# A written order of the early instructions on all five engines of a three-stage attention and mixture kernel

## The chip, the cores and the metric

The kernel runs on 1 core of one Trainium2 chip, with TensorE (PE), VectorE (DVE), ScalarE (ACT), GpSimd (POOL) and SyncE (SP, which issues the transfers). The metric is device time in microseconds of one execution. The kernel before took 881.34 us in the median of three runs (880.27 to 882.56).

## The reference: what is computed

Three stages follow each other on 3072 tokens of width 384.

```python
# 1: gated linear attention, 4 batches x 8 heads, 768 steps, head width 48
S = a * S + k v^T          # a is complex, its magnitude clipped at 0.999; S starts at 0
y = q . Re(S)
# 2: a gated product, weights 384x1536, 384x1536 and 1536x384, given in float64
x = ((y @ w_a) * (y @ w_b)) @ w_out
# 3: top-1 of 8 experts for tokens with x @ w_skip > 0
out = x + gate * (relu(x @ w1[e]) @ w2[e])
```

## The kernel before

**Units and groups.** The attention is cut into 24 units: 6 chunks of 128 steps times 4 batches. Two units make a group of 256 tokens, so that there are 12 groups. The names below carry the unit's or the group's number.

**A unit of attention** goes through `att_exp` (L195), `att_trig` (L238) and `att_pe` (L290). The first clamps `re` on DVE, takes logarithms and exponentials on ACT in the tiles `t1` and `t2`, sums them along the steps on PE (`l2`) and scales `q`, `k` and `im`. The second takes the angle (`t4`), sums it on PE (`tp`), reduces it on DVE (`t3`) and takes sine and cosine on ACT (`ts`, `t4`); products with these give `qr` and `kr` on DVE (L284, L286). The third transposes them on PE (`pq`, `pk`, copied by ACT to `tq`, `tk`), makes the masked scores (`pc`, then `sc` on DVE, L334), the change of the state (`ds`, `state`) and the output `y`. ACT and DVE write `y` as a high and a low half into `xt`, the input of the gated product (L364, L365).

**Weights of the gated product** come as float64: 18 chunks of 768 KB, `rawa0` to `rawa5`, `rawb0` to `rawb5` and `rawo0` to `rawo5`. `decode` (L371) makes float32 of a chunk with one Abs on ACT (L376) and three instructions on DVE (L377, L381, L382); `split` (L386) writes the high half on ACT (L387) and the low half on POOL (L388). Only three decode buffers go round, so that a chunk waits until the chunk three before it has been split. A one-element copy on POOL (L423) holds back the load of chunk k+3 until chunk k is decoded. Chunks of `w_out` are also transposed and multiplied by the gate's columns (`wt`, `wtt`, `w2s`).

**The gated product** of group g and slice f is `ab{g}_{f}`: 18 matmuls of 256 columns on PE (L500 to L502), then `asb` (ACT L506, DVE L507), `gh` (ACT L509), `gl` (DVE L511), and six matmuls into `op{g}_0` and `op{g}_1` (L484 to L486). Routing and the experts of stage 3 follow, and are not touched.

**What sets the order.** The string `START` says in which order the pieces of the first two groups are written down. From that the framework's scheduler puts one order on each engine, by its own estimate of durations. A table `HOLD` of 19 entries bends this: an entry such as `('tab', 2): ('tk', 0, 1)` makes one instruction (the third load of a function table) stand behind another (the copy `tk0_1`) on its engine. Each engine works through its own order strictly, and waits for data of others by semaphores.

Of the kernel before, what the change touches and what calls it, by code (L numbers as in the profile page):

```python
# [3 lines left out]

# [44 lines left out]
IM_MAX = 0.93  # L49
SPL = 4  # L50
OFF = {'add': (0, 1, 2, 3), 'k': (0, 1, 2, 3, 6), 'qs': (5, 6, 7), 'ks': (), 'im': (5,), 'kc': (5,)}
HOLD = {('tab', 2): ('tk', 0, 1), ('shl', 2): ('kr', 1), ('abs', 1): ('tk', 1, 0), ('re', 4): ('sc', 5, 0), ('mx', 3): ('qr', 2), ('shl', 5): ('sc', 3, 0), ('im', 4): ('sc', 4, 0), ('abs', 12): ('ts', 0), ('abs', 4): ('ts', 0), ('shl', 7): ('qr', 1), ('im', 5): ('qr', 5), ('abs', 15): ('tq', 5, 0), ('abs', 9): ('ts', 3), ('abs', 17): ('ts', 1), ('shl', 8): ('sc', 4, 1), ('im', 1): ('qr', 4), ('tab', 6): ('tq', 0, 1), ('tab', 3): ('tk', 5, 1), ('im', 6): ('qr', 4)}
WARMS = (10, 6, 24)
WARMX = (13, 8)
ENGINES = {getattr(mybir.EngineType, x) for x in ("PE", "Activation", "DVE", "Pool")}
# [1 line left out]
SGN = ()  # L57
WO = DM + 10
SKIP_IDX = 8192.0


def kern(tc, q, k, v, a_re, a_im, w_a, w_b, w_out, w_skip, w_gate, w1, w2, out):
    nc = tc.nc
    dve, act, pool, pe, sync = nc.vector, nc.scalar, nc.gpsimd, nc.tensor, nc.sync
    st = ExitStack()
    with st:
# [19 lines left out]
        tri_f = gpool.tile([P, P], F32, tag="xt0", name="tri_f", bufs=1)  # L86
        pool.memset(tri_f, 1.0)
        pool.affine_select(out=tri_f, in_=tri_f, pattern=[[1, P]], compare_op=ALU.is_ge, fill=0.0, base=0, channel_multiplier=-1)
        tri_r = cpool.tile([P, P], F32R, name="tri_r")
        dve.tensor_copy(tri_r, tri_f)  # L90
        tri = tri_r.bitcast(F32)
        if SPL:
            trit = cpool.tile([P, P], F32, name="trit")
            dve.tensor_scalar(out=trit, in0=tri, scalar1=INV2PI, scalar2=None, op0=ALU.mult)
        b_eps = cpool.tile([P, 1], F32, name="b_eps")
        pool.memset(b_eps, LN_EPS)
        b_tiny = cpool.tile([P, 1], F32, name="b_tiny")
        pool.memset(b_tiny, 1e-30)
        b_magic = cpool.tile([P, 1], F32, name="b_magic")
        pool.memset(b_magic, MAGIC)  # L100
        b_hpi = cpool.tile([P, 1], F32, name="b_hpi")
        pool.memset(b_hpi, math.pi / 2)
        immax = cpool.tile([P, 2 * NG], F32, name="immax")
# [30 lines left out]
        def after(later, earlier, how=mybir.DependencyClass.NoSync):  # L134
            tc.add_manual_dep(
                later, earlier.name,
                mybir.DependencyInfo(how, mybir.DependencyReason.DATA),
                reason="table order",
            )


        marks, holds = {}, dict(HOLD)

# [248 lines left out]
        wg = cpool.tile([P, NCC, 10], F32, name="wg")  # L392
# [153 lines left out]
        xd = dpool.tile([NTOK, DM], F32, name="xd")  # L546
# [127 lines left out]
        iota = cpool.tile([P, CAP], BF16, name="iota")  # L674
        pool.iota(iota, pattern=[[1, CAP]], base=0, channel_multiplier=0, allow_small_or_imprecise_dtypes=True)
        desc = cpool.tile([P, NE], F32, name="desc")
        pool.iota(desc, pattern=[[-1, NE]], base=NE, channel_multiplier=0, allow_small_or_imprecise_dtypes=True)
        ones = cpool.tile([P, P], BF16, name="ones")
        pool.memset(ones, 1.0)
        ustrict = cpool.tile([P, P], BF16, name="ustrict")  # L680
        pool.memset(ustrict, 1.0)
        pool.affine_select(out=ustrict, in_=ustrict, pattern=[[1, P]], compare_op=ALU.is_gt, fill=0.0, base=0, channel_multiplier=-1)
        ohs = cpool.tile([P, NE], BF16, name="ohs")
        pool.memset(ohs, 0.0)
        tbl = cpool.tile([P, 2 * 6 * NE], F32, name="tbl")
        pool.memset(tbl, 0.0)

        rt_c = cpool.tile([P, 2 * NG, 6], BF16, name="rt_c")
# [3 lines left out]
        rt_oh = cpool.tile([P, 2 * NG, NE], BF16, name="rt_oh")  # L692
        rt_r = cpool.tile([P, 2 * NG, 6, NE], BF16, name="rt_r")
# [3 lines left out]
        def indices(count_only=False):  # L697
# [4 lines left out]

            dve.tensor_scalar(out=gi, in0=ti[:, :, 0], scalar1=SKIP_IDX, scalar2=None, op0=ALU.add)
            dve.scalar_tensor_tensor(out=gi, in0=ti[:, :, 1], scalar=-SKIP_IDX, in1=gi, op0=ALU.mult, op1=ALU.add)
            dve.tensor_copy(siu, gi)
# [184 lines left out]
        for w in START.split():  # L890
            n = [int(x) for x in w[1:].split(".")] if w[1:] and w[0] != "d" else []
# [24 lines left out]
        for g in range(2, NG):  # L916
# [14 lines left out]
            if g >= NG - 2:  # L931
                for r in sorted(lgs):
                    route(r)

        good = cpool.tile([P, 2], F32, name="good")
        red = cpool.tile([P, 2], F32, name="red")
        cnt = cpool.tile([P, 1], F32, name="cnt")
# [114 lines left out]
        def load_value(x, most):  # L1052
            return nc.values_load(todo[0:1, x : x + 1], min_val=0, max_val=most, skip_runtime_bounds_check_because=why)  # L1053

        left = load_value(2, NTOK // CAP + 1)
        with tc.If(left != 0, label="rest"):
# [5 lines left out]
            n = load_value(0, NTOK // CAP)  # L1062
# [39 lines left out]
```

## Time and profile before

| what | value |
|---|---|
| median of three runs | 881.34 us |
| profiled execution, its own time | 882.94 us |
| span of the profiled execution | 881.0 us |
| PE busy | 829.3 us (94%) |
| DVE busy | 552.9 us (63%) |
| ACT busy | 463.6 us (53%) |
| POOL busy | 266.9 us (30%) |
| mean granted clock of TensorE | 0.98 |

The span is cut into 40 slices on the page, each of 22 us; a digit is the busy share in tenths. An idle time of an engine is put down to the instruction whose result ended it. Durations of neighbouring instructions on DVE and ACT overlap by some hundredths of a microsecond, so that their sum can exceed the busy time of a window.

### The profile page before, as it was taken

To read this page: it belongs to the slowest core of one execution; us is meant where nothing else is said; L and a number is where in the kernel's file an instruction comes from. 1 tells how busy PE (TensorE), PEld (TensorE's weight loads), DVE (VectorE), ACT (ScalarE), POOL (GpSimd) and SP (SyncE) were. 2 spreads that over 40 slices of the span, in tenths; PEclk is the share of its full clock that TensorE was granted. 3 is DMA by queue.
4 is the path that set the end of the run, shared out by engine and by line. 5 is a ranking of instruction groups with operands and counts; after the bars stand their busy time and mean duration, and the time that the engine had idled before them with its cause. 6 is when DMAs were issued, how large, how long until landed. Compare 5 with 4: busy or idle time off the path is not lost. (4 is left out here: it accounts for less than half of the span.)

```text
span 881.0 us, 19344 instructions
## 1 busy us (share of the span) xinstructions
PE 829.3 (94%) x7643; PEld 798.3 (91%) x7643; DVE 552.9 (63%) x1294; ACT 463.6 (53%) x977; POOL 266.9 (30%) x313
## 2 busy tenths in 40 slices
PE   2678879999999999999999999999999999999995
PEld 0568869999999999999999999999999989999995
DVE  4989996639476493855838558394653645655551
ACT  6768664637356472654726546374443425555540
POOL 5464570213031210313103130031201414665741
PEclk9979888999999999999999999999999999999999
DMA  9656532304122040321303222020101419766600
GB/s 217 146 159 168 164 92 54 73 11 96 33 69 51 16 103 19 73 47 47 73 19 76 44 64 56 19 74 10 47 1 41 140 49 327 246 220 215 192 14 30
DMA packets 159923, 79.23 MB, mean 90 GB/s; under 512 B 131060, under 2 KB 147002, under 8 KB 159824
## 3 DMA queue, kind: packets, MB, share of 16 engines
q1 hardware_dynamic: 157776, 72.52, 31.6%
q0 software_dynamic: 2048, 5.40, 1.7%
q8 instruction: 62, 1.02, 0.5%
q14 instruction: 37, 0.30, 0.1%
HBM read 66.10 MB, written 12.61 MB: 89 GB/s over the span
## 5 line engine op out<-in xcount | busy, mean ns | idle before, releaser
L500 PE MATMUL ab<-xt,wa 128*128 128x256 f32 x432 | 125.2, 290 | 5.5 <-DVE asb L507 3.2
L500 PE MATMUL ab<-xt,wb 128*128 128x256 f32 x432 | 124.9, 289 | 0.0
L501 PE MATMUL ab<-xt,wb 128*128 128x256 f32 x432 | 124.1, 287 | 0.0
L501 PE MATMUL ab<-xt,wa 128*128 128x256 f32 x432 | 123.6, 286 | 0.0
L502 PE MATMUL ab<-xt,wb 128*128 128x256 f32 x432 | 123.3, 285 | 0.0
L502 PE MATMUL ab<-xt,wa 128*128 128x256 f32 x432 | 122.7, 284 | 0.0
L507 DVE TENSOR_TENSOR asb<-ab,asb 128x256 f32<-128x256 f32 x144 | 60.0, 417 | 79.3 <-ACT asb L506 79.1
L484 PE MATMUL op<-wo,gl 128*128 128x394 f32 x288 | 99.9, 348 | 4.4 <-DVE gl L511 4.4
L485 PE MATMUL op<-wo,gh 128*128 128x394 f32 x288 | 99.6, 346 | 0.6 <-POOL wo L388 0.6
L486 PE MATMUL op<-wo,gh 128*128 128x394 f32 x288 | 99.9, 347 | 0.0
L509 ACT ACTIVATE gh<-asb 128x256 fp32r<-128x256 f32 x144 | 59.7, 415 | 70.2 <-DVE asb L507 69.8
L506 ACT ACTIVATE asb<-ab 128x256 f32<-128x256 f32 x144 | 54.3, 377 | 77.5 <-PE ab L502 76.1
L500 PEld LDWEIGHTS ab<-xt,wa 128*128 128x128 f32 x432 | 82.6, 191 | 6.3 <-ACT xt L364 2.5
L511 DVE TENSOR_TENSOR gl<-asb,gh 128x256 fp32r<-128x256 f32 x144 | 65.6, 456 | 33.8 <-ACT gh L509 33.5
L500 PEld LDWEIGHTS ab<-xt,wb 128*128 128x128 f32 x432 | 82.9, 192 | 1.2 <-issue 1.2
L502 PEld LDWEIGHTS ab<-xt,wb 128*128 128x128 f32 x432 | 83.0, 192 | 0.5 <-issue 0.4
L501 PEld LDWEIGHTS ab<-xt,wa 128*128 128x128 f32 x432 | 82.9, 192 | 0.5 <-issue 0.5
L501 PEld LDWEIGHTS ab<-xt,wb 128*128 128x128 f32 x432 | 82.9, 192 | 0.4 <-issue 0.4
L502 PEld LDWEIGHTS ab<-xt,wa 128*128 128x128 f32 x432 | 82.6, 191 | 0.3 <-issue 0.3
L753 POOL TENSOR_TENSOR wq<-stg,wq 128x768 fp32r<-128x768 f32 x32 | 59.6, 1864 | 46.7 <-issue 25.8
L792 DVE SCALAR_TENSOR_TENSOR hl<-eh,hh 128x256 fp32r<-128x256 f32 x64 | 27.1, 424 | 52.9 <-ACT hh L791 52.9
L791 ACT ACTIVATE hh<-eh 128x256 fp32r<-128x256 f32 x64 | 24.6, 384 | 67.3 <-PE eh L788 67.3
(232 smaller groups left out, 2177.7 us busy)
## 6 DMA issues: line engine op xcount, KB each, us to landing
stg<-in_moe_w_dram SPq DMA_DIRECT2D x28, 768.0 KB
re<-in_a_re_dram SPq DMA_DIRECT2D x24, 192.0 KB
v<-in_v_dram SPq DMA_DIRECT2D x24, 192.0 KB
k<-in_k_dram SPq DMA_DIRECT2D x24, 192.0 KB
q<-in_q_dram SPq DMA_DIRECT2D x24, 192.0 KB
rawa<-in_moe_w_a_dram SPq DMA_DIRECT2D x6, 768.0 KB
rawb<-in_moe_w_b_dram SPq DMA_DIRECT2D x6, 768.0 KB
rawo<-in_moe_w_out_dram SPq DMA_DIRECT2D x6, 768.0 KB
```

The costliest lines, as they stand in the source:

```text
L484: pe.matmul(o, gl[:, ts], wh, start=f == 0, stop=False)
L485: pe.matmul(o, gh[:, ts], wl, start=False, stop=False)
L486: i = pe.matmul(o, gh[:, ts], wh, start=False, stop=f == NF - 1)
L500: pe.matmul(o, wl, xt[:, c, 0], start=c == 0, stop=False)
L501: pe.matmul(o, wh, xt[:, c, 1], start=False, stop=False)
L502: pe.matmul(o, wh, xt[:, c, 0], start=False, stop=c == NCC - 1)
L506: act.activation(out=asb, in_=ab[:, :256], func=AF.Copy)
L507: dve.tensor_tensor(out=asb, in0=ab[:, 256:], in1=asb, op=ALU.mult)
L509: act.activation(out=gh, in_=asb, func=AF.Copy)
L511: dve.tensor_tensor(out=gl, in0=asb, in1=gh, op=ALU.subtract)
L753: lo.tensor_tensor(out=o[:, 1], in0=t, in1=o[:, 0], op=ALU.subtract)
L792: vm = dve.scalar_tensor_tensor(out=gl, in0=o, scalar=0.0, in1=gh, op0=ALU.max, op1=ALU.subtract)
```

## The change

`HOLD` is emptied. A table `ORDER` lists, for each of the five engines, the tiles that its early instructions write, in the order wanted; `ds0*16` stands for sixteen instructions and `wg:1` for the one with index 1. `keep_rows`, called once behind the loop over the groups, finds the instructions of each name and makes each stand behind the one listed before it on the same engine. These are orders alone, with no new wait between engines. The lists reach from the first load to the start of the third group's gated product. Behind them the scheduler decides as before. No instruction is added, removed or resized.

```diff
+import re
...
-HOLD = {('tab', 2): ('tk', 0, 1), ('shl', 2): ('kr', 1), ('abs', 1): ('tk', 1, 0), ('re', 4): ('sc', 5, 0), ('mx', 3): ('qr', 2), ('shl', 5): ('sc', 3, 0), ('im', 4): ('sc', 4, 0), ('abs', 12): ('ts', 0), ('abs', 4): ('ts', 0), ('shl', 7): ('qr', 1), ('im', 5): ('qr', 5), ('abs', 15): ('tq', 5, 0), ('abs', 9): ('ts', 3), ('abs', 17): ('ts', 1), ('shl', 8): ('sc', 4, 1), ('im', 1): ('qr', 4), ('tab', 6): ('tq', 0, 1), ('tab', 3): ('tk', 5, 1), ('im', 6): ('qr', 4)}
+HOLD = {}
...
+ORDER = {
...
+    "SP": "rawb0 re0 im0 re1 im1 rawa0 rawb1 q0 q1 k1 k0 v1 v0 rawo1 re2 rawo0 ee0:1 ee0:0 re3 im2 im3 k2 ee1*2 carry0 rawa1 k3 v3 wg:1 carry1 rawa2 wg:0 v2 q2 q3 rawo2 rawb2 ee2*2 re4 re5 im4 rawa3 k4 rawb3 rawo3 q4 q5 im5 rawa4 rawb4 rawo4 k5 ee3:1 rawo5 rawb5 v4 carry2 rawa5 v5 ee3:0 imp6:1 imp6:0 re6 re7 cr4 carry3 ee4:1 ee4:0 cr5 ee5:1 xd:1 xd:0 ee5:0 carry4 k6 cr6 q6 carry5 k7 q7 v6 v7 cr7 imp10*2",
+}
+
+def keep_rows(nc, after):
+    writers = {}
+    for i in nc.all_instructions():
+        for o in list(i.outs)[:1]:
+            t = getattr(getattr(o, "bass_ap", None), "tensor", None)
+            if t is not None:
+                writers.setdefault((i.engine, re.sub(r"_\d+$", "", t.name)), []).append(i)
+        if type(i).__name__ == "InstLoadActFuncSet":
+            writers.setdefault((i.engine, "tab"), []).append(i)
+    for engine, words in ORDER.items():
+        used, last = {}, None
+        for w in words.split():
+            w, _, n = w.partition("*")
+            w, _, k = w.partition(":")
+            k, n = int(k or used.get(w, 0)), int(n or 1)
+            for i in writers[getattr(mybir.EngineType, engine), w][k : k + n]:
+                if last is not None:
+                    after(i, last)
+                last = i
+            used[w] = k + n
...
             if g >= NG - 2:
                 for r in sorted(lgs):
                     route(r)
+
+        keep_rows(nc, after)
```

**The first place is the start of DVE's list.** Before, in the kernel's first 20 us, DVE has only attention work and the chunk `deca0`:

```order
L205 TENSOR_SCALAR re0_137,remin_87<-re0_137 128x384
L210 TENSOR_REDUCE immax_86<-im0_139 128x1
L205 TENSOR_SCALAR re1_144,remin_87<-re1_144 128x384
L210 TENSOR_REDUCE immax_86<-im1_146 128x1
L213 SCALAR_TENSOR_TENSOR t1_0_199<-t1_0_199,t2_0_200 128x384
L224 TENSOR_TENSOR im0_139<-im0_139,t2_0_200 128x384
L213 SCALAR_TENSOR_TENSOR t1_1_223<-t1_1_223,t2_1_224 128x384
L224 TENSOR_TENSOR im1_146<-im1_146,t2_1_224 128x384
L377 TENSOR_SCALAR deca0_187<-deca0_187 128x768
L263 TENSOR_SCALAR t3_0_248<-tp_0_251 128x384
L381 SCALAR_TENSOR_TENSOR deca0_187<-rawa0_177,deca0_187 128x768
L264 SCALAR_TENSOR_TENSOR t3_0_248<-t3_0_248,tp_0_251 128x384
```

Now it begins with the decode of `rawb0`, and the chunks `deca0` and `decb1` stand between the steps of the first two units:

```order
L412 TENSOR_SCALAR decb0_461<-decb0_461 128x768
L416 SCALAR_TENSOR_TENSOR decb0_461<-rawb0_181,decb0_461 128x768
L417 SCALAR_TENSOR_TENSOR decb0_461<-rawb0_181,decb0_461 128x768
L240 TENSOR_SCALAR re0_137,remin_87<-re0_137 128x384
L240 TENSOR_SCALAR re1_144,remin_87<-re1_144 128x384
L245 TENSOR_REDUCE immax_86<-im0_139 128x1
L248 SCALAR_TENSOR_TENSOR t1_0_199<-t1_0_199,t2_0_200 128x384
L248 SCALAR_TENSOR_TENSOR t1_1_223<-t1_1_223,t2_1_224 128x384
L412 TENSOR_SCALAR deca0_187<-deca0_187 128x768
L416 SCALAR_TENSOR_TENSOR deca0_187<-rawa0_177,deca0_187 128x768
L245 TENSOR_REDUCE immax_86<-im1_146 128x1
L259 TENSOR_TENSOR im1_146<-im1_146,t2_1_224 128x384
```

What moved: the three instructions of `decb0` stand ahead of the clamp of `re0`; in SP's list the load of `rawb0` stands ahead of all others too. Behind the rows shown come the multiplication of `im0`, the three of `decb1` with the last of `deca0` between, and then the `t3` of both units.

**The second place is DVE's list around the last instructions for the slices 8 and 9 of group 0** (`gl0_9`, `gl0_8`). Before:

```order
L507 TENSOR_TENSOR asb0_8_1324<-ab0_8_1299,asb0_8_1324 128x256
L447 COPY w2s5_1276<-wt5_0_1277 128x10
L235 TENSOR_TENSOR k5_1122<-k5_1122,t2_5_1476 128x384
L511 TENSOR_TENSOR gl0_9_1266<-asb0_9_1261,gh0_9_1264 128x256
L511 TENSOR_TENSOR gl0_8_1329<-asb0_8_1324,gh0_8_1327 128x256
L235 TENSOR_TENSOR k4_1111<-k4_1111,t2_4_1447 128x384
L447 COPY w2s5_1276<-wt5_1_1287 128x10
L210 TENSOR_REDUCE immax_86<-imp6_2140 128x1 x2
L250 SCALAR_TENSOR_TENSOR t4_4_1506<-cr4_1508,t4_4_1506 1x384
```

Now:

```order
L352 TENSOR_TENSOR state3_94<-ds3_892,ee3_623 96x8x48
L546 TENSOR_TENSOR gl0_9_1266<-asb0_9_1261,gh0_9_1264 128x256
L546 TENSOR_TENSOR gl0_8_1329<-asb0_8_1324,gh0_8_1327 128x256
L542 TENSOR_TENSOR asb0_10_1372<-ab0_10_1347,asb0_10_1372 128x256
L542 TENSOR_TENSOR asb1_0_1406<-ab1_0_1381,asb1_0_1406 128x256
L546 TENSOR_TENSOR gl0_10_1377<-asb0_10_1372,gh0_10_1375 128x256
L542 TENSOR_TENSOR asb0_11_1438<-ab0_11_1413,asb0_11_1438 128x256
L245 TENSOR_REDUCE immax_86<-im5_1118 128x1
L245 TENSOR_REDUCE immax_86<-im4_1107 128x1
L482 COPY w2s5_1276<-wt5_1_1287 128x10
L259 TENSOR_TENSOR im4_1107<-im4_1107,t2_4_1447 128x384
L546 TENSOR_TENSOR gl1_0_1411<-asb1_0_1406,gh1_0_1409 128x256
```

What moved: `im4`, the reductions of `im4` and `im5`, and the multiplication of `k5` (one of the rows before) stood ahead of `gl0_8` and now stand behind it, as do the clamps of `re6` and `re7`. They belong to units 4 to 7.

**The third place is PE's list at the same point.** Before, the six matmuls of `gl0_9` and the six of `gl0_8` stand ahead of the product `ab0_10`:

```order
L190 MATMUL l2_4_1458<-ll4_1460,tri_r_74 128x384
L191 MATMUL l2_4_1458<-lh4_1459,tri_r_74 128x384
L484 MATMUL op0_0_551<-wo4_1210,gl0_9_1266 128x394
L485 MATMUL op0_0_551<-wo4_1210,gh0_9_1264 128x394
L486 MATMUL op0_0_551<-wo4_1210,gh0_9_1264 128x394
L484 MATMUL op0_1_552<-wo4_1210,gl0_9_1266 128x394
L485 MATMUL op0_1_552<-wo4_1210,gh0_9_1264 128x394
L486 MATMUL op0_1_552<-wo4_1210,gh0_9_1264 128x394
```

Now PE's list has there the six matmuls of `gl0_6`, of which the last four rows stand here, and then nine matmuls of `ab0_10`:

```order
L521 MATMUL op0_0_551<-wo3_1025,gh0_6_1198 128x394
L519 MATMUL op0_1_552<-wo3_1025,gl0_6_1200 128x394
L520 MATMUL op0_1_552<-wo3_1025,gh0_6_1198 128x394
L521 MATMUL op0_1_552<-wo3_1025,gh0_6_1198 128x394
L477 MATMUL wt5_1_1287<-ident_66,deco5_1268 128x128 x3
L535 MATMUL ab0_10_1347<-xt0_367,wa5_1336 128x256
L536 MATMUL ab0_10_1347<-xt0_367,wa5_1336 128x256
L537 MATMUL ab0_10_1347<-xt0_367,wa5_1336 128x256
```

What moved: behind the nine of `ab0_10` come the 18 matmuls of `ab1_0`, three of `wt5_1`, the other nine of `ab0_10`, and only then those of `gl0_9`. The sums `l2_4` and `l2_5`, which stood ahead of the matmuls of `gl0_9`, stand later too, behind the products `ab1_4` and `ab1_1`.

## Rows read from the trace of the kernel before

**Rows 1.** The page: busy tenths of PE in 40 slices of 22 us.

```profile
PE   2678879999999999999999999999999999999995
```

**Rows 2.** Busy time by windows: us, PE, PEld, DVE, ACT, POOL, PEclk, DMA share, GB/s.

```profile
0.00:19.00 19.00, 4.57 (x6) 1.84 (x7) 7.50 (x13) 12.36 (x22) 11.79 (x38) 1.00 1.10 217
19.00:53.00 34.00, 22.85 (x207) 15.96 (x205) 30.27 (x45) 22.03 (x38) 14.06 (x15) 0.95 0.72 170
53.00:75.00 22.00, 19.93 (x127) 17.89 (x128) 20.24 (x33) 19.05 (x38) 15.01 (x14) 0.84 0.43 127
75.00:132.00 57.00, 46.37 (x407) 43.09 (x405) 56.83 (x75) 37.29 (x72) 33.89 (x33) 0.89 0.51 143
...
140.00:200.00 60.00, 60.00 (x607) 59.04 (x606) 35.83 (x96) 33.11 (x75) 9.32 (x13) 1.00 0.18 41
```

**Rows 3.** Waits of PE between 0 and 145 us: in total, times, longest.

```profile
PE l L218 <- DVE t L213: 11.5, 2, 9.5
...
PE op L484 <- DVE gl L511: 3.8, 2, 2.1
```

**Rows 4.** DVE's timeline, 24 to 50 us: start, duration, instruction.

```profile
24.21 2.15 DVE L286 TENSOR_TENSOR kr<-k,ts 128x384 f32<-128x384 f32 x1
...
35.33 0.55 DVE L286 TENSOR_TENSOR kr<-k,ts 128x384 f32<-128x384 f32 x1
...
36.26 2.13 DVE L377 TENSOR_SCALAR decb<-decb 128x768 int32<-128x768 int32 x1
...
39.59 0.94 DVE L381 SCALAR_TENSOR_TENSOR decb<-rawb,decb 128x768 int32<-128x768 int32 x1
...
44.66 2.09 DVE L382 SCALAR_TENSOR_TENSOR decb<-rawb,decb 128x768 int32<-128x768 int32 x1
```

**Rows 5.** POOL's instructions in the timeline of the first 40 us.

```profile
12.72 1.20 POOL L234 TENSOR_TENSOR q<-q,t 128x384 f32<-128x384 f32 x1
...
16.31 0.99 POOL L235 TENSOR_TENSOR k<-k,t 128x384 f32<-128x384 f32 x1
...
23.95 2.00 POOL L388 TENSOR_TENSOR wa<-deca,wa 128x768 fp32r<-128x768 f32 x1
...
35.90 1.99 POOL L388 TENSOR_TENSOR wo<-deco,wo 128x768 fp32r<-128x768 f32 x1 [0.45 <-ACT wo L387]
```

**Rows 6.** The first load in the timeline, and what follows it, 0 to 23 us.

```profile
0.81 0.43 SPq L177 DMA_DIRECT2D re<-in_a_re_dram  x1
...
3.97 0.55 DVE L205 TENSOR_SCALAR_CACHE_REDUCE re<-re 128x384 f32<-128x384 f32 x1
...
18.76 0.90 ACT L376 ACTIVATE decb<-rawb 128x768 f32<-128x768 f32 x1
18.89 0.56 DVE L377 TENSOR_SCALAR deca<-deca 128x768 int32<-128x768 int32 x1 [3.58 <-ACT deca L376]
...
21.82 0.51 ACT L155 ACTIVATE ts<-t 128x384 f32<-128x384 f32 x1
```

**Rows 7.** Timelines of POOL and DVE, 60 to 70 us, and of DVE, 90 to 98 us.

```profile
64.90 1.82 POOL L388 TENSOR_TENSOR wa<-deca,wa 128x768 fp32r<-128x768 f32 x1
...
65.78 0.54 DVE L210 TENSOR_REDUCE immax<-im 128x1 f32<-128x384 f32 x1
...
91.88 2.07 DVE L224 TENSOR_TENSOR im<-im,t 128x384 f32<-128x384 f32 x1
...
95.33 0.54 DVE L205 TENSOR_SCALAR_CACHE_REDUCE re<-re 128x384 f32<-128x384 f32 x1
```

**Rows 8.** The timeline of all engines, 128 to 141 us.

```profile
127.43 0.86 DVE L235 TENSOR_TENSOR k<-k,t 128x384 f32<-128x384 f32 x1
...
128.22 3.01 DVE L511 TENSOR_TENSOR gl<-asb,gh 128x256 fp32r<-128x256 f32 x2
...
130.29 0.70 PE L484 MATMUL op<-wo,gl 128*128 128x394 f32 x1 [2.12 <-DVE gl L511]
```

**Rows 9.** The window of the last half clock before the end, columns as in Rows 2.

```profile
129.40:139.60 10.20, 9.31 (x37) 9.31 (x38) 4.74 (x7) 2.44 (x4) 3.63 (x5) 0.50 0.41 78
```

4 rows, old and new, of the table ORDER are left out of this document.

## The prediction

> **What bounds the kernel now.** I read the slices of PE first. PE is full from the seventh slice on, and holes are left in the first 140 us and at the very end [rows 1]. The change touches the first 200 us only, so the question is how much of the early holes it closes. Next come the busy times by windows [rows 2]. In the first 19 us DVE works 7.50 us and stands idle 11.5. From 19 to 53 us it is idle for 34.00 - 30.27 = 3.7 us, from 53 to 75 us for 22.00 - 20.24 = 1.8 us, and from 75 to 132 us for 0.2 us. PE has 57.00 - 46.37 = 10.6 us of holes in that last window. From 140 to 200 us PE is full and DVE has 24.2 us to spare. So up to some 132 us the early part is bound by DVE, and behind it by PE. The waits of PE say the same: 11.5 us go to the first two sums, which DVE releases, and the last long wait of the part is for `gl` on DVE [rows 3]. It ends at 130.29 us with `gl0_9` [rows 8].
>
> DVE's time is not all work. `kr` takes 2.15 us beside a split of 2.00 us on POOL, and 0.55 us where POOL is quiet; the shift of `decb` takes 2.13 us beside the split that starts at 35.90 us, and the same shift of `deca` 0.56 us [rows 4 to 6]. An instruction that meets a split thus waits for most of it.
>
> **The change, part by part.** The measure is the moment at which DVE is through with `gl0_9` and `gl0_8`, and PE's backlog then. Everything behind it is PE's own work, and the change leaves its amount alone.
>
> 1. *Decodes move into the idle front.* The six DVE instructions of `decb0` and `decb1` stand at 36.26 to 46.75 us now, where DVE has hardly a gap [rows 4]. In the new list they stand in the first 20 us. Unhindered they are two shifts of 0.56 us and four steps of 0.94 us, 4.9 us; as traced, with the two long ones, 0.94 x 3 + 0.54 + 2.13 + 2.09 = 7.6 us (0.94 is the row, its two like rows and the second shift of 0.54 are not shown). Against this, 768 KB go ahead of the first attention load: at 217 GB/s [rows 2] that is 3.6 us by which all attention inputs come later. The gain lies between 4.9 - 3.6 = 1.3 and 7.6 - 3.6 = 4.0 us. I take the middle, 2.6, since whether the long ones become short depends on what POOL does then.
> 2. *Idle time between 19 and 75 us.* 3.7 + 1.8 = 5.5 us are idle there. The new list puts a decode or the work of another unit between the steps of a chain that passes through ACT and PE and back, on most of these places. Between nothing and 5.5 I take half, 2.7; the trace does not show which of the new neighbours are ready.
> 3. *Work moved behind `gl0_8`.* `im4` (2.07 us), the reductions of `im4` and `im5` (one row of 0.54, the other alike), the clamps of `re6` and `re7` (0.54, one shown) and the multiplication of `k5` (0.86) leave the path [rows 7, 8]: 2.07 + 4 x 0.54 + 0.86 = 5.1 us. With `im4` at 0.55 us, the price of such a row without POOL, it is 3.6. I take 5.1, because POOL's multiplication of `im5` and both `ll` leave that stretch as well. They are hidden later: DVE has 24.2 us to spare from 140 to 200 us [rows 2], and needs 5.1 of them. If that cover were gone, the sums `tp_4` and `tp_5` would be the late ones.
> 4. *PE's order at the end of the part.* Now PE stands still for 2.12 us until `gl0_9` is there [rows 8]. In the new list 9 + 18 + 3 + 9 matmuls stand ahead of its six, and none of them needs `gl0_9`. This wait of 2.1 us goes, and what is late next is the conversion of the last weights, `wa5` and `wb5`. Bounds: 0 (the weights are as late as `gl0_9`) and 2.1; I take 2.1.
>
> The other reorderings of ACT, POOL and SP I cost at nothing: ACT is busy 37.29 of 57 us and POOL 33.89 [rows 2], and each load still stands behind the same one-element copy. On SP each waiting load holds up those behind it; the new list puts `carry0` and the `ee` loads ahead of loads of weights. ACT's and POOL's results for those are there when they are asked for, as far as the order shows. If not, the decode three chunks later is late.
>
> The sum against the profiled execution: 882.94 - 2.6 - 2.7 - 5.1 - 2.1 = 870.4 us. That execution is 1.6 us above the median of the runs, so I forecast 881.34 - 12.5 = **868.8 us**. With all lower bounds (1.3 + 0 + 3.6 + 0 = 4.9) it is 876.4. With all upper ones (4.0 + 5.5 + 5.1 + 2.1 = 16.7) it is 864.6. [...] The lowest end is then 864.6 - 4.7 = 859.9.
>
> **The rivals.** *DVE and POOL collide more often* (0.15). Now four multiplications of `q` and `k` on POOL, 1.20 + 3 x 0.99 = 4.2 us, run while DVE is idle or at the edge of it [rows 5]. In the new order DVE has decodes there, and the splits of `wb0` and `wa0` (2.00 us each) move in beside them. If all of it holds DVE up as the split held up `kr`, 4.2 + 4.0 = 8.2 us are given back: 868.8 + 8.2 = 877.0 us. For it speaks the row of `kr`; against it, that DVE's instructions on PSUM and its reductions keep their length beside splits (the reduction of 0.54 us at 65.78 us, while a split runs from 64.90 us [rows 7]). [...]
>
> *Slower: the chain of the first units sets the pace, not DVE's load* (0.12). The first load is issued at 0.81 us and DVE clamps `re0` at 3.97 [rows 6]. With 3.6 us of weights ahead, of which the weights themselves land 0.9 us before `re0` (192 KB at 217 GB/s), `rawb0` is there at 3.97 + 2.7 = 6.7 us. The Abs adds 0.90 us, the three steps 2.4 us, and the clamp of `re0` starts at 10.0 instead of 3.97, 6.0 us later. If nothing behind it makes this up, the kernel takes 881.3 + 6.0 = 887.3 us. For it speaks that PE's first wait is the longest of all [rows 3]; against it, that DVE has no gap for 57 us after 75 us, so a delay of the front is lost in its queue. It decides if the sine of the first unit, which starts at 21.82 us now, starts behind 26 us.
>
> *The moved work comes back* (0.07). Units 4 and 5 are late, and PE stands still for the 5.1 us between 140 and 200 us, with the 2.1 of part 4: 868.8 + 7.2 = 876.0 us. Against it: DVE is idle 40% of that window.
>
> **How the numbers follow.** The forecast has 0.66. Its own range is 859.9 to 876.4; the first and third rival lie at 877.0 and 876.0, and the slower one at 887.3. From 860 to 880 us some 0.61 of the forecast, 0.13 of the first rival and 0.06 of the third are held, 0.80 in all. A measurement of this kernel can tell about 0.3%, 2.6 us, from no change. Below 878.7 us lie the forecast, the third rival and a little more than half of the first: 0.80. Within 2.6 us of before lie the rest of the first and a slower front that is partly made up: 0.08. Slower: 0.12.
>
> **What would show it.** Right, if DVE's idle time in the first 19 us falls from 11.5 to about 8 us, `gl0_8` ends near 121 us instead of 131.2, and PE is full from then on to 200 us. Part 1 is wrong if the decodes of `rawb0` and `rawb1` take more than 6 us in the front. Part 2 is wrong if DVE still has 5 us of gaps between 19 and 75 us. Part 3 is wrong if PE waits for `tp`, `pk5` or `xt2` behind 130 us. Part 4 is wrong if PE waits for the splits of `wa5` or `wb5` as long as it did for `gl0_9`. The whole is wrong if PE's last early wait ends at 130 us or later.

## The result, and the profile after

The changed kernel takes **866.54 us** in the median (865.25 to 866.85, 4 runs), the kernel before 881.14 us (880.27 to 882.56, 4 runs, on the same chip). The ratio is 0.983 (95% interval 0.9813 to 0.9847): 14.6 us less. The profiled execution took 866.85 us, its span is 865.1 us. The trace has one ACT instruction more than before, a function-table load (26 instead of 25).

The slices of PE on the page, of the changed kernel:

```profile
PE   1889999999999999999999999999999999999995
```

PE is at nine tenths or more from the fourth slice on but for the last, where it was from the seventh [rows 1]. The busy times by windows, of the changed kernel (columns as in rows 2); the last two are the only stretches of half clock before the last microseconds:

```profile
0.00:19.00 19.00, 2.93 (x4) 1.17 (x4) 10.72 (x19) 13.33 (x22) 6.68 (x21) 1.00 1.02 225
19.00:53.00 34.00, 27.66 (x252) 20.76 (x252) 31.64 (x44) 27.96 (x48) 24.91 (x31) 1.00 0.75 178
53.00:75.00 22.00, 18.87 (x111) 16.91 (x111) 19.26 (x31) 14.74 (x31) 15.07 (x16) 0.77 0.68 187
75.00:132.00 57.00, 54.04 (x507) 51.29 (x508) 48.63 (x80) 38.81 (x77) 29.50 (x35) 1.00 0.43 116
140.00:200.00 60.00, 58.12 (x587) 56.25 (x586) 42.46 (x117) 34.12 (x77) 13.09 (x18) 1.00 0.25 54
54.43:57.84 3.41, 3.41 (x10) 2.08 (x10) 2.56 (x7) 2.58 (x6) 3.41 (x3) 0.50 1.18 275
64.67:71.49 6.82, 6.18 (x25) 5.99 (x26) 5.49 (x9) 4.39 (x10) 2.22 (x4) 0.50 0.73 230
```

The waits of PE in the first 200 us, of the changed kernel (in total, times, longest). The first is longer than before, the wait for `gl` is nearly gone [rows 3]:

```profile
PE l L253 <- DVE t L248: 15.1, 1, 15.1
PE pc L367 <- ACT tk L364: 3.8, 4, 1.7
...
PE op L519 <- DVE gl L546: 1.1, 2, 0.8
```

**Where the span's 15.9 us came from, on PE.** Its busy time fell from 829.3 to 820.8 us, 8.5 us, and its idle time by 7.4 us. By the estimate below, the busy time fell because work ran at full clock instead of half. Before, five stretches had a granted clock of 0.50, one of them [rows 9], and these four:

```profile
44.02:47.43 3.41, 3.41 (x48) 2.74 (x46) 3.41 (x6) 0.64 (x1) 2.37 (x2) 0.50 0.55 208
54.26:61.08 6.82, 5.47 (x23) 4.77 (x23) 6.75 (x10) 5.96 (x10) 5.62 (x5) 0.50 0.36 118
91.80:98.63 6.83, 6.29 (x51) 5.54 (x52) 6.83 (x10) 4.11 (x8) 4.51 (x6) 0.50 0.58 178
122.52:125.94 3.42, 3.42 (x17) 3.32 (x17) 3.39 (x6) 2.48 (x6) 2.06 (x2) 0.50 0.03 10
```

With 9.31 us of [rows 9] PE was busy for 27.9 us at half clock before, and for 3.41 + 6.18 = 9.6 us now. Half the clock doesn't double the time here: the products of 256 columns start every 0.214 us in the stretch of [rows 9] and every 0.117 us between 140 and 150 us, where the clock was full. By these two figures the difference of 18.3 us takes 10.0 us at full clock. The estimate of 8.3 us saved is about what the busy time fell by.

**Where DVE's time went.** `gl0_8` ended at 131.2 us and ends now at 115.27 + 2.68 = 117.95 us, 13.3 us earlier. DVE's idle time up to there has hardly changed: 17.2 us before, 16.7 now. Its busy time fell by 12.8 us. I took for each form of instruction the lower quartile of its durations as its plain length, and summed what exceeds it by over 0.2 us. Up to `gl0_8`, before, 29 of 155 instructions were stretched, by 29.7 us in all; now it is 22 of 149, by 19.3 us. So 10.4 of the 13.3 us are stretches that are gone. From 75 us on, where it counts most, the sum fell from 18.6 us (16 of 71) to 6.2 us (7 of 61). Each of these 23 rows overlaps an instruction of POOL. Two of them, before, in the timeline of POOL and DVE:

```profile
112.24 1.70 POOL L388 TENSOR_TENSOR wo<-deco,wo 128x768 fp32r<-128x768 f32 x1
...
112.52 1.84 DVE L377 TENSOR_SCALAR deco<-deco 128x768 int32<-128x768 int32 x1
113.91 2.16 POOL L388 TENSOR_TENSOR wb<-decb,wb 128x768 fp32r<-128x768 f32 x1
114.40 2.50 DVE L381 SCALAR_TENSOR_TENSOR deco<-rawo,deco 128x768 int32<-128x768 int32 x1
```

And a split in the changed kernel, with what DVE has beside it:

```profile
93.75 0.68 DVE L369 TENSOR_TENSOR sc<-pc,tri_r 128x512 f32<-128x512 f32 x1
...
94.04 1.86 POOL L423 TENSOR_TENSOR wa<-deca,wa 128x768 fp32r<-128x768 f32 x1
94.36 0.54 DVE L240 TENSOR_SCALAR_CACHE_REDUCE re<-re 128x384 f32<-128x384 f32 x1
```

The shift of 0.56 us takes 1.84 us beside the first split, the step of 0.94 us takes 2.50 beside the second. In the new list an instruction that reads PSUM (`sc`) and a clamp stand there (`sc` starts just before the split, the clamp inside it), and both keep their length, 0.68 and 0.54 us, which are the lower quartiles of their forms. In these rows the two that are stretched are a step with two SBUF inputs and a plain shift.

The two traces as a whole say the same. I counted the DVE instructions up to `gl0_8` that start inside a multiplication or a split on POOL (0.05 us or more behind its start, with 0.6 us or more of it still to run). Of those with two SBUF inputs, or a plain shift, there were 24 before and there are 14 now; 36 of these 38 are stretched by more than 0.2 us. Of PSUM readers, reductions and clamps there were 13 and there are 26; none of the 39 is stretched. So DVE meets POOL about as often as before, 40 times against 37, and the order puts the kinds there that keep their length.

**The first product.** `ab0_0` starts at 46.2 us instead of 53.4. Before, five rows of the timelines of PE, SP and ACT make the chain:

```profile
47.29 0.37 SPq L417 DMA_DIRECT2D rawa<-in_moe_w_a_dram  x1
...
47.88 0.85 PE L353 MATMUL y<-sc,v 128*32 128x128 f32 x20
...
52.08 0.89 ACT L376 ACTIVATE deca<-rawa 128x768 f32<-128x768 f32 x1 [2.79 <-DMA rawa<-in_moe_w_a_dram]
52.87 0.48 ACT L364 ACTIVATE xt<-y 128x384 fp32r<-128x384 f32 x1
...
53.40 0.51 PE L500 MATMUL ab<-xt,wa 128*128 128x256 f32 x2 [2.24 <-ACT xt L364]
```

The load of `rawa1` is let go when `decb1` is decoded, at 44.66 + 2.09 = 46.75 us [rows 4]. ACT stands still until it lands, and the copy of `y` into `xt` waits behind it on ACT, though `y1` had been ready since 47.88 + 0.85 = 48.7 us. Now, the four of SP, ACT and PE:

```profile
33.27 0.40 SPq L452 DMA_DIRECT2D rawa<-in_moe_w_a_dram  x1
...
42.18 0.94 ACT L411 ACTIVATE deca<-rawa 128x768 f32<-128x768 f32 x1
...
44.38 0.49 ACT L399 ACTIVATE xt<-y 128x384 fp32r<-128x384 f32 x1 [0.48 <-PE y L388]
...
46.18 0.37 PE L535 MATMUL ab<-xt,wa 128*128 128x256 f32 x1
```

### The profile page after: what moved, and what is told of

It reads as the page before. It is cut to its first block, busy times and chain, and to the rows that moved or that the text cites. A ratio compares the mean times of both kernels' runs of the same rounds, so it can differ in the third digit from the quotient of the medians.

```text
span 865.1 us, 19360 instructions
## 1 busy us (share of the span) xinstructions
PE 820.8 (95%) x7643; PEld 790.3 (91%) x7643; DVE 545.1 (63%) x1294; ACT 465.1 (54%) x978; POOL 266.3 (31%) x313
## 4 chain that ended last, share of the span: by engine, by line
PE 84%; DVE 5%; DMA 3%; issue 2%; ACT 2%; POOL 2%; POOLq 0%; SPq 0%; ACTq 0%; DVEq 0%
PE ab L535 11%; PE ab L536 10%; PE ab L537 10%; PE op L519 6%; PE op L521 5%; PE op L520 5%; PE y L388 5%; PE pc L367 5%; PE eh L820 3%; PE pq L357 3%; PE eh L823 3%; PE eh L821 3%; PE eo L837 3%; PE eo L839 3%; PE eo L838 3%; PE pk L362 2%
## 5 line engine op out<-in xcount | busy, mean ns | idle before, releaser
L535 PE MATMUL ab<-xt,wb 128*128 128x256 f32 x432 | 124.0, 287 | 0.0
L536 PE MATMUL ab<-xt,wb 128*128 128x256 f32 x432 | 122.3, 283 | 0.0
L537 PE MATMUL ab<-xt,wb 128*128 128x256 f32 x432 | 121.5, 281 | 0.0
L535 PEld LDWEIGHTS ab<-xt,wa 128*128 128x128 f32 x432 | 81.7, 189 | 3.7 <-DVE asb L542 3.2
L535 PEld LDWEIGHTS ab<-xt,wb 128*128 128x128 f32 x432 | 81.4, 188 | 1.1 <-issue 1.0
L536 PEld LDWEIGHTS ab<-xt,wa 128*128 128x128 f32 x432 | 81.7, 189 | 0.6 <-issue 0.5
L537 PEld LDWEIGHTS ab<-xt,wb 128*128 128x128 f32 x432 | 81.4, 189 | 0.4 <-issue 0.4
L536 PEld LDWEIGHTS ab<-xt,wb 128*128 128x128 f32 x432 | 81.4, 188 | 0.4 <-issue 0.4
L537 PEld LDWEIGHTS ab<-xt,wa 128*128 128x128 f32 x432 | 81.5, 189 | 0.0
```

The source lines that it names most:

```text
L535: pe.matmul(o, wl, xt[:, c, 0], start=c == 0, stop=False)
L536: pe.matmul(o, wh, xt[:, c, 1], start=False, stop=False)
L537: pe.matmul(o, wh, xt[:, c, 0], start=False, stop=c == NCC - 1)
```

## The experiments

Twelve kernels ran, each four to ten times. "Against the change" compares a median with 0.983 times the median of the kernel before in the same sitting; a difference under some 2 us is not told apart.

| run | median, us | ratio to before (95%) | against the change |
|---|---|---|---|
| pad ahead of the front | 871.12 | 0.988 (0.9859 to 0.9902) | +3.8 |
| pad ahead of `gl0_9` | 870.71 | 0.9869 (0.9847 to 0.9891) | +3.4 |
| pad behind `gl0_8`, one block | 872.45 | 0.9881 (0.9854 to 0.9907) | +5.1 |
| pad behind `gl0_8`, in gaps | 867.17 | 0.9833 (0.9808 to 0.9858) | +0.6 |
| PE's old end | 874.26 | 0.9909 (0.9891 to 0.9927) | +6.9 |
| no list for PE | 874.57 | 0.9915 (0.9886 to 0.9943) | +7.3 |
| units first | 866.95 | 0.983 (0.981 to 0.9851) | -0.3 |
| decodes back | 879.37 | 0.9965 (0.9945 to 0.9984) | +12.1 |
| lists to 45 us only | 869.92 | 0.9867 (0.9845 to 0.9888) | +2.6 |
| front alone, on before | 882.05 | 0.998 (0.9957 to 1.0002) | +14.9 |
| scheduler alone | 880.54 | 0.9983 (0.9966 to 1.0) | +13.4 |
| filled holes | 865.15 | 0.9796 (0.9773 to 0.9819) | -2.0 |

For the runs that keep the change's order of PE, one can also say by how much a tile's last matmul ends later (+) than in the trace of the change:

| tile (its end in the change, us) | front pad | pad at `gl0_9` | block behind | in gaps | old end | units first | decodes back | filled |
|---|---|---|---|---|---|---|---|---|
| `y1` (44.31) | +4.33 | -0.07 | -0.05 | -0.10 | +0.09 | +0.28 | +3.53 | -0.11 |
| `ab0_1` (51.98) | +4.38 | -0.01 | +0.02 | -0.04 | +0.06 | +0.28 | +12.09 | -0.14 |
| `ab0_8` (109.91) | +3.39 | -2.10 | +0.56 | -1.11 | -1.68 | +0.39 | +10.87 | -1.88 |
| `ab0_11` (121.41) | +3.41 | +1.80 | +0.56 | -1.12 | +6.69 | +0.37 | +10.85 | -1.91 |
| `ab1_8` (131.82) | +3.37 | +1.77 | +4.90 | -1.15 | +6.68 | +0.39 | +10.85 | -1.92 |
| `ab4_8` (325.94) | +3.40 | +1.82 | +5.00 | -0.02 | +7.71 | +0.20 | +11.89 | -1.97 |

What a run has lost or won by 132 us, it keeps to within 1.2 us until 326 us. PE has few holes there in which it could be made up, 1.9 us from 140 to 200 us in the change. The three runs that lose 1.0 to 1.1 us more on that way (in gaps, old end, decodes back) each have a stretch of 3.4 us at half clock between 180 and 196 us, which the change lacks (its clock from 140 to 200 us is 1.00, that of the last two 0.97). The same order can also shift by 1 to 2 us between 52 and 110 us with nothing changed there (second, fourth and fifth column). In the second and fifth the half clock falls into other stretches, and fewer of them (from 53 to 75 us the clock is 0.84 in both, 0.77 in the change); in the fourth its stretches are as long as in the change, and its 1.1 us stay open. A single trace can't tell less than that.

### Where DVE has slack: four pads

Ten reductions whose result nobody reads are listed at one place of DVE's list. They took 4.68 us. A memset on POOL fills their source once; the list lines are shown in part.

```diff
+        padsrc = cpool.tile([P, W], F32, name="padsrc")
+        pool.memset(padsrc, 0.5)
+        padr = cpool.tile([P, 16], F32, name="padr")
+        for j in range(10):
+            dve.tensor_reduce(out=padr[:, j : j + 1], in_=padsrc, axis=AX.X, op=ALU.max)
...
-    "DVE": "tri_r trit decb0*3 re0 re1
+    "DVE": "tri_r trit decb0*3 padr*10 re0 re1
```

> The changed kernel with ten extra reductions of 128x384 on DVE (some 0.46 us each by the pitch of two neighbouring reductions in the trace, 4.6 us in all) between the decode of rawb0 and the clamp of re0. Theory (DVE's load bounds the early part, so a delay of the front is lost in its queue): at most 1.5 us slower, 866.5 to 868.0 us. Rival (the chain of the first units sets the pace): 4.6 us slower, 871.1 us.

The second has `state3 padr*10 gl0_9`, the third `gl0_10 asb0_11 padr*10 immax:5`:

> The same ten reductions (4.6 us) directly ahead of gl0_9 on DVE, at 115.3 us of the changed kernel's trace. Theory (DVE is the path until gl0_8, which is part 3 of the prediction): the whole 4.6 us come out, 871.1 us, and more (up to 2 us) if TensorE's clock falls to half behind the wait. Rival (PE has spare work enough behind gl0_9): under 1.5 us, 866.5 to 868.0 us.

> The same ten reductions (4.6 us) directly behind asb0_11 on DVE, some 4 us behind gl0_8, at the place to which the change moved im4 and the reductions. Theory of the prediction (work behind gl0_8 is hidden): under 1.5 us, 866.5 to 868.0 us. Rival (products of group 1 wait for asb1_4, since only two product banks go round, so that DVE still sets the pace there): 2.6 to 4.6 us slower, 869.1 to 871.1 us.

The last puts one or two at a time into gaps: `w2s5 padr*2 im4`, `k4 padr lg0 t4_4 lg0 padr tl4`, `gl1_8 padr t3_5`, `re7 padr*2 sc4_0`, `asb1_5 padr sc4_1 kr5 padr state0`, `xt2 padr asb1_7`.

> The ten extra reductions (4.6 us) again behind gl0_8 on DVE, but one or two at a time at eight places between 123 and 155 us where the changed kernel's trace shows DVE idle: ahead of im4, lg0, tl4, t3_5, sc4_0, sc4_1, state0 and asb1_7. Theory (work behind gl0_8 is hidden if it lies in DVE's gaps; the block of ten cost 4.3 us because it stood ahead of products that PE waits for): at most 1 us slower than the change, 866.5 to 867.5 us. Rival (DVE sets the pace there in any case): 3 to 5 us slower, 869.5 to 871.5 us.

**Front:** 3.8 us slower, and the table shows 4.33 us at `y1`, of which 3.4 stay. The theory that a delay of the front is lost in DVE's queue fell; the run with the units first, below, shows why. **Ahead of `gl0_9`:** the table goes from -2.10 to +1.80, 3.9 us, so a place ahead of `gl0_9` is on the path. But the whole 4.6 us, which the theory expected, do not come out. Three rows of the timelines of DVE and PE of that run, and PE's window behind them:

```profile
113.19 4.67 DVE L140 TENSOR_REDUCE padr<-padsrc 128x1 f32<-128x384 f32 x10
117.79 0.74 DVE L546 TENSOR_TENSOR gl<-asb,gh 128x256 fp32r<-128x256 f32 x2
...
118.24 1.02 PE L519 MATMUL op<-wo,gl 128*128 128x394 f32 x2 [2.25 <-DVE gl L546]
```

```profile
118.19:121.60 3.41, 3.36 (x12) 3.36 (x13) 1.51 (x5) 1.07 (x3) 0.00 (x0) 0.50 0.00 0
```

`gl0_9` and `gl0_8` together take 0.74 us now, where they take 2.68 in the change: POOL is through with its last split and its `ll` at 115.4 us in this run, before the two start, and works beside them in the change, where the split runs from 114.49 to 116.51 us and the `ll` from 116.48 to 117.67. So 1.9 us of the pad are won back there. What PE loses is a wait of 2.25 us and, by my estimate from the two intervals of the products, 1.5 us by the half clock behind it, 3.8 us in all.

**One block behind `gl0_8`:** from +0.56 to +4.90, 4.3 us. So a place behind `gl0_8` isn't free in itself. What PE waited for is not what the rival named. Three rows of the timelines of DVE and PE of that run:

```profile
122.77 4.68 DVE L140 TENSOR_REDUCE padr<-padsrc 128x1 f32<-128x384 f32 x10
...
128.29 0.15 DVE L482 COPY w2s<-wt 128x10 f32<-128x10 f32 x1
...
129.49 0.63 PE L519 MATMUL op<-wo,gl 128*128 128x394 f32 x2 [1.48 <-ACT wo L422]
```

The pad held back a copy of 0.15 us, `w2s5`, from which ACT and POOL make the last columns of `wo5`, and PE's next matmuls read these; waits of 1.14 us and 0.67 us (`asb`) follow. The first of these is put down to a memset on POOL which stands right behind POOL's split of `wo5` (129.51 + 1.69 = 131.20 us), so it is that split. The last the change has too. Then 3.4 us of PE's work run at half clock, from 133.4 us, some 1.5 us more by the same estimate. The two new waits and this make 4.1 of the 4.3 us. **The same work in gaps** costs nothing (0.6 us by the medians, -1.15 us in the trace). What is hidden behind `gl0_8` is work in pieces that nobody waits behind.

### PE's list: the old end, and no list

```diff
-    wt5_1*3 ab0_10*9 ab1_0*18 wt5_1*3 ab0_10*9 op0_0 op0_1 op0_0*2 op0_1*2 ab0_11*18 ab1_4*18 l2_4*2 op0_0*3 op0_1*3
+    wt5_1*3 op0_0 op0_1 op0_0*2 op0_1*2 op0_0*3 op0_1*3 ab0_10*9 ab1_0*18 wt5_1*3 ab0_10*9 ab0_11*18 ab1_4*18 l2_4*2
```

> Part 4 undone alone: PE's matmuls with gl0_9 and gl0_8 stand ahead of ab0_10 again, all else as in the change. By the prediction's term 2.1 us slower (868.6 us). By the times of the changed trace PE would stand still from 113.1 until gl0_8 at 118.0 and have 2.4 us of work less behind it: 3.7 us slower (870.2 us). If the clock falls to half behind that wait as in the kernel before, up to 4.7 us more (875 us). Rival (the list of PE at that place is worth nothing, something later is late anyway): under 1 us.

> The change with the list of PE emptied, the other four kept; the scheduler orders PE. If the order of PE counts as the run with PE's old end says: at least 4 us slower, 870.5 us or more. If the four other lists carry the gain and PE's order follows from them: within 1.5 us of the change, 865 to 868 us.

6.9 us slower. PE's waits from 108 to 122 us in that run, and then its window at half clock:

```profile
PE op L519 <- DVE gl L546: 3.8, 1, 3.8
```

```profile
113.34:120.17 6.83, 4.94 (x17) 4.97 (x18) 2.88 (x3) 1.53 (x4) 2.60 (x2) 0.50 0.45 85
```

The wait of 3.8 us is back, and with it a stretch of half clock that the change doesn't have: 4.94 us of work at half clock are some 2.2 us more, by the same estimate. Two shorter waits follow, 0.9 us (`asb`) and 1.1 us (`kr` on POOL by the profile). That is the pattern of [rows 8] and [rows 9] before. With no list for PE it is 7.3 us; there PE's longest wait from 75 to 132 us is one of 3.0 us for `sc`. PE's order counts, and most of what it is worth lies in not standing still.

### The front: units first, decodes back, front alone, lists to 45 us

```diff
-    "SP": "rawb0 re0 im0 re1 im1 rawa0 rawb1
+    "SP": "re0 im0 re1 im1 rawb0 rawa0 rawb1
...
-    "DVE": "tri_r trit decb0*3 re0 re1 immax t1_0 t1_1 deca0*2 immax im1 im0 decb1
+    "DVE": "tri_r trit re0 re1 immax immax t1_0 t1_1 decb0*3 im1 im0 deca0*2 decb1
```

> The change with re0, im0, re1, im1 loaded ahead of rawb0 again, and the decode of rawb0 on ACT and DVE behind the first attention steps (all still in the first 20 us). Theory A (found from the extra reductions in front: a shift of the first units comes out at the end by four fifths): the first sum starts some 4 to 5 us earlier than 15.1 us, and the kernel is 1.5 to 3.5 us faster than the change, some 863 to 865 us. Theory B (the prediction's: DVE's load sets the pace, a delay of the front is lost in its queue): within 1 us of the change, 865.5 to 867.5 us. Rival C (the weights set the pace, and rawb0 comes later now): slower than the change by 1 to 3 us.

No difference, as theory B says. The first sums end 3.7 us earlier, and nothing of it is left at `y1`. Four rows of DVE's timeline of that run show where it went:

```profile
15.60 2.45 DVE L416 SCALAR_TENSOR_TENSOR deca<-rawa,deca 128x768 int32<-128x768 int32 x1
17.97 1.09 DVE L412 TENSOR_SCALAR decb<-decb 128x768 int32<-128x768 int32 x1
...
20.82 1.77 DVE L417 SCALAR_TENSOR_TENSOR decb<-rawb,decb 128x768 int32<-128x768 int32 x1
22.52 0.54 DVE L298 TENSOR_SCALAR t<-tp 128x384 f32<-128x384 f32 x1
```

The decodes stand ahead of `t3_0`, which starts at 22.5 us as in the change (22.6). So DVE's load sets the pace there, and not the first load's arrival. In the change the two end almost together; its row of `t3_0`:

```profile
22.62 0.56 DVE L298 TENSOR_SCALAR t<-tp 128x384 f32<-128x384 f32 x1 [0.38 <-PE tp L288]
```

DVE waits there 0.38 us for the chain of the first unit. An earlier arrival can gain no more than that, and a pad ahead of the chain, as in the front, delays it at once (4.33 us at `y1`).

Decodes back (`rawb0` and `rawb1` loaded and decoded where the kernel before has them; their splits and the chunk `rawo1` move with them, all behind some 50 us is as in the change):

```diff
-    "SP": "rawb0 re0 im0 re1 im1 rawa0 rawb1 q0 q1 k1 k0 v1 v0 rawo1 re2
+    "SP": "re0 im0 re1 im1 q0 q1 k1 k0 v1 v0 rawa0 rawb1 rawb0 re2
...
-    deco0 state0 immax:3 immax:2 deco1 t1_3
+    deco0 state0 decb0*3 immax:3 immax:2 decb1*3 t1_3
```

> Part 1 undone alone: rawb0 and rawb1 are loaded behind the attention inputs of units 0 and 1, and decoded on DVE behind state0, ahead of t1_3, as in the kernel before; the chunk rawo1, which needs the buffer of rawb0's decode, moves behind them; all lists behind some 50 us stay. By the prediction's term 2.6 us slower than the change (1.3 to 4.0): 869.1 us. Theory A (the gain of 7 to 11 us that PE shows between 36 and 61 us comes from weights that are ready when the first products can start): 5 to 10 us slower, 871.5 to 876.5 us. Rival (the earlier start of the units pays for it): not slower than the change.

12.1 us slower, more than any theory said. The waits of ACT (19 to 62 us) and of PE (30 to 62 us) in that run:

```profile
ACT deca L411 <- DMA rawa<-in_moe_w_a_dram: 4.6, 1, 4.6
ACT deco L411 <- DMA rawo<-in_moe_w_out_dram: 3.6, 1, 3.6
```

```profile
PE l L253 <- DVE xt L400: 6.8, 1, 6.8
```

It is the chain of the first product again: late decode, late load, ACT stands still, `xt` is late. At `ab0_1` this run is 12.09 us behind the change, and the kernel before 12.32 us. My layout adds a delay of its own: in SP's list the load of `rawa1` stands behind that of `v2`, which waits for `y` on PE. `rawa1` could have gone at 44.04 us and went at 48.37, so up to 4.3 us of the lateness come from that place. No run has `rawa1` ahead of `v2`. So 12.1 us is what these lists lose without their front, not a price of six instructions.

Front alone: the kernel before, with the lists' first 20 us for ACT, DVE, POOL and SP and its table of entries but `('abs', 1)` and `('shl', 2)`:

```diff
+    "DVE": "tri_r trit decb0*3 re0 re1 immax t1_0 t1_1 deca0*2 immax im1 im0 decb1 deca0 decb1*2",
...
+    "SP": "rawb0 re0 im0 re1 im1 rawa0 rawb1 q0 q1 k1 k0 v1 v0",
```

> The kernel before with its table of 19 entries (without the two that hold back the decodes of rawb0 and rawb1), and of the new lists only the first 20 us of ACT, DVE, POOL and SP: rawb0 loaded first, rawb0 and rawb1 decoded in the idle front. PE has no list. All behind it is the scheduler's. By the prediction's part 1: 2.6 us faster than before, 878.7 us. Theory A (weights ready in time are worth 11 us by 62 us, and that stays to the end): 868 to 873 us. Rival (the new front disturbs what the entries were made for): not faster than before, 881 us or more.

No gain at all; theory A and part 1 both fell in this form. Four rows of DVE's timeline of that run:

```profile
39.60 0.95 DVE L417 SCALAR_TENSOR_TENSOR deco<-rawo,deco 128x768 int32<-128x768 int32 x1
...
41.34 0.68 DVE L369 TENSOR_TENSOR sc<-pc,tri_r 128x512 f32<-128x512 f32 x1
41.94 2.11 DVE L417 SCALAR_TENSOR_TENSOR deca<-rawa,deca 128x768 int32<-128x768 int32 x1
44.13 0.69 DVE L369 TENSOR_TENSOR sc<-pc,tri_r 128x512 f32<-128x512 f32 x1
```

With its chunks released early, the scheduler decodes `rawo0`, `rawo1` and `rawa1` ahead of the first unit's scores: `sc0_1` starts at 44.1 us instead of 34.7, and `y1` ends 19.1 us later than in the change. What the front saves is spent on weights that aren't wanted yet. The clock differs beside it. The ten executions of this kernel took 874.9 to 882.9 us; the trace is of one with a mean granted clock of 0.969, and the two with the highest, 0.986 and 0.988, took 874.9 and 878.6 us, one with 0.982 took 881.9. No run tells what the front alone is worth at the change's clock.

> The five lists end at some 45 us of the changed kernel's trace (behind y1 on PE, xt0 on DVE); behind that the scheduler decides alone, without the table of 19 entries. Theory A (most of the gain is made by 65 us): 869 to 873 us. Rival (parts 3 and 4, at the end of the early part, carry it): 875 us or more.

> No list and no table: the scheduler's own order on all engines. It tells what the front lists alone add (the run with the lists of the first 45 us had 869.9 us with the same scheduler behind them). Theory A (early decodes carry the gain): 10 us or more slower than that run, 880 to 890 us, with the first products waiting until 53 us or later. Rival (the 19 entries of the table did harm, and leaving them out is what gained): 873 us or less.

With all five lists to 45 us and the scheduler alone behind them: 869.9 us, 2.6 us from the whole change. With no list: 880.5 us, as before. So about 10.6 of 13.4 us come with the first 45 us of the lists, once decodes and units are ordered together, and theory A's place is right, if not its reason. The lists of ACT, POOL and SP were never taken away singly, so what each of them is worth stays open.

### The half clock that is left

```diff
+                if n == [0, 0]:
+                    env.fill = [pe.matmul(M[0][1][0][:, 400:], ident, ident[:, :112], start=True, stop=True).ins for x in range(23)]
...
-    ab0_1*9 wt0_1*3 tp_2
+    ab0_1*9 fill*8 wt0_1*3 tp_2
...
-    wt1_0*3 wt1_1*3 pq2_0*4 pk2_0*4 pc2_0*4
+    wt1_0*3 fill*5 wt1_1*3 fill*5 pq2_0*4 pk2_0*4 fill*5 pc2_0*4
```

> The change with 23 extra matmuls of 112 columns on PE, whose results nobody reads, in the four holes at 52.0, 60.9, 62.5 and 64.6 us, ahead of and between the two stretches of half clock (54.4 to 57.8 and 64.7 to 71.5 us). If they keep the clock full and PE's own work sets the pace from there: the 3.41 and 6.19 us of busy time at half clock lose half, up to 4.8 us, of which 2 to 4 come out, 862.5 to 864.5 us. If DVE's path hides it: within 1 us of the change. If the filling itself is in the way or does not move the clock: 0 to 1.5 us slower.

The window of that run, where the change has 18.87 us at 0.77:

```profile
53.00:75.00 22.00, 20.77 (x164) 18.93 (x163) 20.34 (x32) 14.59 (x31) 15.30 (x16) 1.00 0.70 188
```

In this execution no half clock is left until 860 us (mean granted clock 0.998), and PE is 1.9 us ahead of the change from `ab0_8` to `ab4_8`. The other three executions had 0.993, which the change's fastest also had (865.25 us), and took 864.7 to 865.6 us, no longer than the profiled one (865.9 us). So the filling did not keep the clock up each time, and the gain is not shown to come from the clock. The medians say 2.0 us, the ratios 0.9796 against 0.983, 3 us; their intervals overlap slightly (up to 0.9819, from 0.9813). So this kernel is some 2 us faster than the change, the least that was expected, and just at what can be told apart.

## Why the prediction was right, and where its steps were wrong

The forecast was 868.8 us, the measurement 866.5. The sum was right by size, its terms were not: parts 1 and 2 gave less in their own places, other things gave more. That they came out at the sum is partly luck.

- **The measure**, `gl0_8`'s end and PE's backlog, held. It was to end near 121 us and ended at 118; and what a run has at 132 us, it keeps to within 1.2 us. PE is not quite full from then on to 200 us.
- **Part 1 (2.6 us) failed as a price.** Its own mark came true: DVE's idle time in the first 19 us fell from 11.5 to 8.3 us, and the six instructions take 5.8 us in the front, under its 6. But it counted DVE's time and the later attention loads alone, not who waits for the load that a decode lets go. That chain runs through the orders of SP and ACT to `xt`, and the prediction put the reorderings of these two at nothing. It cost 12.1 us at the first products when it was undone, up to 4.3 us of them by that run's own layout, and setting the front alone gained nothing.
- **Part 2 (2.7 us) failed** by its mark: the gaps from 19 to 75 us are 34.00 - 31.64 + 22.00 - 19.26 = 5.1 us, where 5.5 were [rows 2].
- **Part 3 (5.1 us)** rests on "hidden behind `gl0_8`". The pads bear that out for work in gaps, and refute it for a block at the same place. Its marks stayed quiet: none of PE's waits behind 130 us is for `tp`, `pk5` or `xt2`. Its size is not confirmed: DVE's plain work up to `gl0_8` fell by 2.4 us only, since other work came in.
- **Part 4 (2.1 us) was too small.** The wait is gone, and putting the old end back costs 6.9 us: 3.8 us of wait, some 2.2 us by the half clock behind it, and two shorter waits. What I had named as late next, the splits of `wa5` and `wb5`, did not hold PE up.
- **The half clock** stood in the sum only as the lowest end: 4.7 us, half of the 9.31 us of [rows 9], one stretch of five. No run shows this term, that such work takes half the time at full clock; by the intervals of the products, 0.214 and 0.117 us, it is 4.2. In the accounting above all the stretches together give 8.3 us of PE's busy time.
- **First rival (DVE and POOL collide more, +8.2 us):** that DVE's instructions stretch beside POOL was right (36 of 38 of the kinds counted above), the sign wrong. Fewer of these kinds meet POOL, 14 instead of 24: 10.4 us less stretching up to `gl0_8`. It is the largest entry of DVE's account. No run changed the collisions alone, so that they cause the gain is read from the trace, not shown by experiment.
- **Slower rival (the chain of the first units):** `ts0` starts at 23.9 us, 2.1 us later than before, under the 26 us from which it decided. The run with the units first shows that an earlier arrival alone gains nothing; DVE's queue ends within 0.4 us of it.
- **Third rival:** PE has 1.9 us of holes from 140 to 200 us, where it had none, instead of the 5.1 feared.

The parts don't add: undone one at a time they cost 12.1 and 6.9 us, more than the 14.6 us of the whole. A written order is worth something as a whole, and a term of it only beside the others.

## What to carry to other kernels

When a step that releases a load moves, follow the load to the engine that waits for it, and then what stands behind that wait in the engine's order; here a copy whose data had been there for some 4 us stood behind it. Price DVE beside POOL by the rows that keep their length (here PSUM readers, reductions and clamps with an accumulator: none of 39 was stretched), and lay those beside POOL's multiplications and splits. Work is hidden when it lies in gaps, not when it merely lies behind the last wait: the same ten reductions cost 0.6 us there, and 5.1 in one block.

## What was not expected of the hardware

In two runs the granted clock stayed at half for long, 27.3 and 34.1 us, while PE was busy most of the time. The windows of the run with the front alone, and of the scheduler alone, at a granted clock of 0.50:

```profile
21.07:48.37 27.30, 18.17 (x107) 12.47 (x108) 26.21 (x34) 17.45 (x29) 16.21 (x15) 0.50 0.77 210
```

```profile
27.85:61.98 34.13, 25.03 (x196) 20.04 (x196) 29.92 (x40) 18.43 (x31) 14.23 (x16) 0.50 0.61 169
```

PE was busy for two thirds and three quarters of them, 18.17 and 25.03 us. In the change it had holes of 1.6 us at most in the 10 us ahead of its first stretch at half clock, and in the profiled execution of the run with the filled holes the clock stayed up (0.998 in the mean); in the other three, at 0.993, it did not do so throughout.
